# Three input loads of a fused RWKV-7 and gated-MLP kernel moved later: a of chunk 5 and b of chunk 4 into chunk 2, b of chunk 5 to the start of chunk 3

## The chip, the cores and the metric

The kernel runs on one core of a Trainium2 chip. The metric is the device time of one execution in microseconds; the kernel before takes 807.01 us (median of three runs, 802.86 to 811.95). The profile is that of one execution, which took 806.77 us. Times given as points, such as "at 86.40", count from the start of its span.

## What is computed

Two blocks run one after the other. The first is a recurrence over 768 time steps, for 4 batches and 8 heads with a head dimension of 40. The second applies two matrix products with x·cos(x) between them to the 3072 token rows that the first puts out.

```python
for t in range(S):
    y[:, :, t] = einsum('bhd,bhde->bhe', r[t], state)
    Sa = einsum('bhde,bhe->bhd', state, a[t])
    state = state * w[t][:, :, None, :] - einsum('bhd,bhe->bhde', Sa, b[t]) \
            + einsum('bhd,bhe->bhde', v[t], k[t])
x = y.transpose(0, 2, 1, 3).reshape(3072, 320)
h = x @ w_in                      # w_in 320 x 2048
out = (h * cos(h)) @ w_out        # w_out 2048 x 320
```

The two weight matrices arrive in double precision, as 8-byte words; the kernel turns them into float32 itself.

## The kernel before, in words

**Chunks.** The recurrence is cut into 24 chunks of 32 steps. A chunk `c` is five segments of `main(c)`, made at lines 921 to 927: `t` (`ch_t`: transposes the state, tile `sT`), `q` (`qps`), `x` (`x0ps`), `s` (`sps`) and `z` (`ch_z`: tile `dps`, then VectorE adds into the state `qz` at L754 and GpSimd multiplies it at L755). The next chunk's `ch_t` needs that `qz`. The three segments `v`, `k` and `g` of `p2(c + 1)` prepare the next chunk. `p1(c)` prepares w, a and b for a pair of chunks: `p1_w` (`pw`), `p1_a` (`pa`), `p1_b` (`pb`), `p1_n` (`pn`).

**Inputs.** Each input has one or two buffers in on-chip memory. `a`, `b` and `w` of chunk 4 go to the buffers that chunk 0 used, those of chunk 5 to the buffers of chunk 1; chunks 2 and 3 have places of their own, so these buffers are free long before chunk 1. `load(c, names)` (lines 146 to 152) issues four DMAs for each name, one for each batch, of 40 KB in runs of 160 bytes. All loads of this stage go through the queue of SyncE (SP), which works in program order: a DMA that waits holds up all behind it.

**Who reads the three loads.** `p1_w(4)`, which is `pw4`, the second segment of chunk 3, calls `over_w(4)`: VectorE takes the reciprocal of w (L395), then GpSimd multiplies b of chunk 4 by it (L396). `p1_a(4)`, which is `pa4`, transposes a of chunks 4 and 5 on TensorE (L330) and calls `over_w(5)`, whose product on GpSimd reads b of chunk 5.

**Weights.** `weights()` cuts the two matrices into 20 blocks of 128 x 512. Each block n goes through four steps (`rounded`, lines 224 to 266): fetch (L237, one to four DMAs on SP into a `words` buffer), taken (VectorE L245 and L246, ScalarE L249 and L251), mantissa (VectorE L255, ScalarE L258) and product (VectorE L261, GpSimd L264). The text below says F10 for the fetch of block 10, T10 for its "taken", M10 and P10 for the other two. From block 10 on there are three buffers in turn, so F10 can start once M7 has read block 7, F11 once M8 is done, F12 once M9 is done. The steps stand in one list, `w_steps`, of which each segment emits some after its own work: four in chunk 1, two in chunk 2, three in chunk 3. The order in the list around the change is P7, F10, M8, T9, P8, F11, M9, T10, P9, F12, M10, T11, P10 and so on.

**Order by hand.** The whole program is emitted in one order, and every engine runs its part of it in order. `step(work)` emits one segment; `later(n, work)` emits `work` behind the n-th step from then. In chunk 1 the steps are `t, F1, v, q, k, S1, x, g, s, z`; in chunk 2 `t, F2, v, q, S2, k, M, x, M, F3, g, M, s, S3, M, z, M, M`, where each M is a piece of the second block (`first_a`, `first_b` or `second`: tiles `ph` and `po`), and the F and S segments with numbers are small pieces of the recurrence (tile `below`). `busy` and `kept_busy` (tile `spare`) emit matmuls whose results nobody reads.

So in chunk 1 the SP queue holds, in this order behind the step named: w of chunk 5 and v of chunk 3 (`k`), a of chunk 5 and r of chunk 3 (`S1`), b of chunk 5 (`x`), F10 (`g`), b of chunk 4 and F11 (`s`), F12 (`z`). T10 stands behind step `s` on VectorE, and so ahead of the state updates L754 of chunk 1's `z`.

Of the kernel before, what the change touches and what calls it, by code (L numbers as in the profile page):

```python
# [20 lines left out]
def kernel(  # L21
# [124 lines left out]
    def load(c, names, via=nc.sync, parts=range(B)):  # L146
        for n in names:
            for i in parts:
                at_c = src[n][i, :, c * C : (c + 1) * C, :]
                if n == "w" and c >= 4:  # L150
                    at_c = wd[c // 4][i, :, c % 4]
                via.dma_start(nat[n, c][blk[i], :, :D], at_c.rearrange("h t d -> t h d"))  # L152
# [190 lines left out]
    def later(steps, work):  # L343
        waiting.append([steps, work])
# [201 lines left out]
    def pair_first(c, i, moe=True):  # L546
        ps = pair_space(c, moe, ps_h, "h")
        nt = G["noff"].rearrange("p c e j t -> p (c e j) t")
        half = pair_half(c, i)
        for n in range(H):  # L550
            for g in range(B):
                mm(
                    ps[blk[g], HB * n : HB * (n + 1)], nt[blk[g], H * i + n, :],
                    G["rn"][blk[g], H * i + n, :], n == 0,
                )
        nc.scalar.copy(half[:, :, :HB], ps[:, : H * HB].rearrange("p (n u) -> p n u", u=HB))
        if c + i == 3:
            nc.gpsimd.memset(padding(bn_b[6]), 0.0)
# [326 lines left out]
    def p1(c):  # L885


        def first_w():
            p1_w(c)
            if c == 4:  # L890
                later(1, lambda: load(6, "w"))

        def both_a():
            p1_a(c)
            if c == 4:
                later(1, lambda: load(7, "w"))
                for n in "ab":
                    for i in range(2):
                        later(1, lambda n=n, i=i: load(6 + i, n))
            elif c > 4 and c + 3 < NCH:  # L900
                for m in range(6):
                    later((9 if c == 6 else 2) + m, lambda m=m: load(c + 2 + m % 2, "wab"[m // 2]))

        return [first_w, both_a, lambda: p1_b(c), lambda: p1_n(c)]

    def scanned(q):

        ws_scan(q)
        later(2, lambda: ws_store(q))
        if q + 1 < NCH // 4:  # L910
            later(12, lambda: ws_fetch(q + 1))

    def p2(c):
        def last():
            p2_g(c)
            if c + 1 < NCH:
                later(4 if c == 1 else 1, lambda: p2_in(c + 1))

        return [lambda: p2_v(c), lambda: p2_k(c), last]

    def main(c):
        def last():
            ch_z(c)
            if c + 2 < NCH:
                later(8 if c == 2 else 1, lambda: p2_kn(c + 2))

        return [lambda: ch_t(c), lambda: ch_q(c), lambda: ch_x(c), lambda: ch_s(c), last]

    with tc.manual_schedule():
# [24 lines left out]
        def busy(n, after=False):  # L954


            ps = ps_h.tile([P, 512], F32, tag="h", name="busy")
            if after:
                nc.vector.memset(tick, 1.0)
                nc.tensor.matmul(  # L960
                    ps[:1, :], lhsT=tick, rhs=pick(idle, 0, (0, 4), (1, P)), start=True, stop=True, skip_group_check=True
                )
            for _ in range(n):
                mm(ps, idle, pick(idle, 0, (0, 4), (1, P)), True)
# [11 lines left out]
        def shifted(n):  # L976


            ps = at("pad")
            for _ in range(n):  # L980
                mm(ps[:1, 0, :1], idle[:, :1], idle[:, :1], True)
# [43 lines left out]
        busy(6)  # L1025
        step(z0, 0, 2)
        busy(4)
        for n, c, name in ((1, 4, "a"), (3, 4, "w"), (5, 5, "w"), (6, 5, "a"), (7, 5, "b"), (9, 4, "b")):
            later(n, lambda c=c, name=name: load(c, name))

        done = 0
# [17 lines left out]
        for c in range(NCH):  # L1049
            t, q, x, s, z = main(c)  # L1050
            v, k, g = p2(c + 1) if c + 1 < NCH else [lambda: None] * 3
            q0 = c - c % 4 + 4
            fill, pn, pn4 = (1, 4), None, None
            if c == 0:
                segs = []
            elif c == 1:
                segs, fill = [t, F1, v, q, k, S1, x, g, s, z], (1, 4)
            elif c == 2:
                segs, fill = [t, F2, v, q, S2, k, M, x, M, F3, g, M, s, S3, M, z, M, M], (0, 2)
            elif c == 3:  # L1060
                pw4, pa4, pb4, pn4 = p1(4)
                pw, pa, pb, pn = p1(6)
                segs = [
                    t, pw4, M, q, pa4, M, x, lambda: scanned(2), M, s, pw, M, pb4, pa, M, pn4, M, z, M,
                    pb, v, pn, k, M, g,
                ]
                fill = (2, 3)
            elif c == 4:
                pw, pa, *p8 = p1(8)
                firsts = [lambda n=n: pair_first(4, n) for n in range(4)]  # L1070
                seconds = [lambda n=n: pair_second(4, n) for n in range(4)]
                F4, F5, F6, F7 = firsts
                S4, S5, S6, S7 = seconds
                segs = [
                    t, v, M, q, M, k, x, M, F4, M, S4, F5, M, s, F6, M, pw, F7, M, z, M, g, M, pa, S5, lambda: scanned(3),
                ]
                fill = (2, 0)
            elif c == 5:
                pw, pa = p1(10)[:2]
                pb, pn = p8  # L1080
                segs = [t, M, pb, q, M, pn, k, M, x, M, s, S6, M, z, M, S7, M, pw, v, M, g, pa, M]
            elif c % 4 == 0 and q0 < NCH:
                pb, pn = p1(q0)[2:]
                segs = [t, v, M, q, M, k, x, M, g, M, s, pb, M, z, M, pn, M, M]
                if q0 + 4 < NCH:
                    segs.insert(-1, lambda: scanned(c // 4 + 2))
            elif c % 4 == 1 and q0 < NCH:
                pw, pa = p1(q0 + 2)[:2]
                segs = [t, M, pw, q, M, x, k, M, s, v, M, z, M, pa, M, g, M, M]
            elif c % 4 == 2 and q0 < NCH:  # L1090
                pb, pn = p1(q0 + 2)[2:]
                segs = [t, M, pb, q, M, pn, v, M, x, M, s, k, M, g, M, z, M, M]
            elif c % 4 == 3 and q0 + 4 < NCH:
                pw, pa = p1(q0 + 4)[:2]
                segs = [t, M, pw, q, M, x, k, M, s, v, M, z, M, pa, M, g, M, M]
            else:
                segs = [t, v, M, q, M, x, k, M, g, M, s, M, M, z, M, M]
            n = len(segs)

            goal = 8 * (c + 1) - (18 if c < 19 else 20)  # L1100
            empty, places = 0, segs.count(M)
            if c > 3:
                empty = max(0, min(places - (goal - done), 2 if c < 8 else places))
                goal = max(goal, done + places - empty)
            place = 0
            if c == 19:
                shifted(N_PAD[c])
            for i, seg in enumerate(segs):
                kept_busy(FILL.get((c, i), 0))
                while seg is s and ("rt", c) not in G:  # L1110
                    if allowed(c):
                        piece(4, 0)
                    else:
                        inv_steps.pop(0)()
                while seg is pn4 and w_steps:
                    w_steps.pop(0)()
                if seg is not M:
                    G["kind"] = "q" if seg is q and c > 3 else "other"
                    step(seg, *((0, 0) if c < 3 and seg in (*firsts, *seconds) else fill), small=seg in (q, x, g, s, z, pn, pn4, *firsts, *seconds))
                    if seg not in (*firsts, *seconds) and (c < 2 or c == 2 and not done):  # L1120
                        busy({s: 6, q: 5, v: 4, k: 4, z: 4}.get(seg, 3))
                else:
                    place += 1
                    if place * empty // places > (place - 1) * empty // places:
                        continue
                    if allowed(c) and (c != 4 or done < 23):
                        piece(*fill)
                while i == n - 1 and c > 3 and done < goal and c != 4 and allowed(c):
                    piece(*fill)
                if seg is pn and (c == 3 or c > 4 and c % 4 == 2):  # L1130
                    inv_steps.extend(by_blocks(q0) if c == 3 else inverse(q0))
# [36 lines left out]
```

## Time and profile before

| what | value |
|---|---|
| median of three runs | 807.01 us (802.86 to 811.95) |
| the profiled execution | 806.77 us |
| its span (first to last instruction) | 805.0 us |
| TensorE busy (PE) | 752.7 us, 94% of the span |
| VectorE busy (DVE) | 487.0 us, 60% |
| ScalarE busy (ACT) | 387.8 us, 48% |
| GpSimd busy (POOL) | 201.1 us, 25% |
| mean granted TensorE clock | 0.973 of full |
| SP's DMA queue | 52.11 MB, 30.1% of the 16 DMA engines' time |

The span is what the trace covers; the execution has 1.77 us around it. The profile's page cuts the span into 40 slices of 20.1 us. In the view "timeline" a line gives start, duration, engine, source line, operation, the tile written and the tiles read, a count, and in brackets the idle time of the engine before it with what ended it. "issue" there means a wait for nothing that the profile shows. SPq is SP's queue of DMA issues; its durations are those of issuing, not of the transfer.

### The profile page before, as it was taken

The numbers are of one execution on the slowest core, as the hardware profiler recorded it, in microseconds if no ns is written. First come the engines' busy times: TensorE is split into PE (matmuls) and PEld (weight loads), VectorE is DVE, ScalarE is ACT, GpSimd is POOL, SyncE is SP. The second block draws the span as 40 slices with busy tenths as digits, with TensorE's granted clock in tenths as the row PEclk, the third lists the DMA queues.
The fourth block names the chain that finished last, engine by engine and source line by source line (L and its number), as shares of the span: only waits on it lengthen the run. The fifth ranks groups of instructions, "written<-read, shape, count | busy, mean of one in ns | idle before, by whom it ended". The sixth has DMA issues, their size and how long they took to land.

```text
span 805.0 us, 39600 instructions
## 1 busy us (share of the span) xinstructions
PE 752.7 (94%) x17812; PEld 575.5 (71%) x17812; DVE 487.0 (60%) x1025; ACT 387.8 (48%) x723; POOL 201.1 (25%) x354
## 2 busy tenths in 40 slices
PE   5777698999999999999999999999999999999997
PEld 4544376777777777777777777777787777777775
DVE  8779658864734796553895644994346873333231
ACT  1337467555425435545435635535645445354352
POOL 5316535320322220330330230332131122201000
PEclk9688799999999999999999999999999999999999
DMA  8666552354253324334214314223220222101000
GB/s 114 176 162 149 143 145 74 57 121 65 59 125 58 66 38 71 72 92 67 60 40 69 94 36 72 53 45 69 46 46 21 46 46 49 24 17 34 19 17 16
DMA packets 183303, 55.78 MB, mean 69 GB/s; under 512 B 157152, under 2 KB 178656, under 8 KB 183136
## 3 DMA queue, kind: packets, MB, share of 16 engines
q1 hardware_dynamic: 177440, 52.11, 30.1%
q8 instruction: 140, 2.29, 1.2%
q10 hardware_dynamic: 5440, 0.82, 0.7%
q0 software_dynamic: 256, 0.33, 0.2%
q14 instruction: 27, 0.22, 0.1%
HBM read 42.07 MB, written 11.14 MB: 66 GB/s over the span
## 4 chain that ended last, share of the span: by engine, by line
PE 66%; DVE 18%; ACT 4%; issue 4%; DMA 3%; SPq 3%; POOL 1%; DVEq 0%; ACTq 0%; POOLq 0%
PE ph L101 23%; PE po L101 19%; PE x0ps L101 3%; PE dps L101 3%; SPq L152 3%; DVE inv_tmp L494 3%; DVE rw L395 3%; PE vT L330 3%; PE gram L101 2%; DVE inv L498 2%; PE sps L101 2%; PE nps L101 2%; PE qps L101 2%; PE sT L654 1%; DMA nat_a<-in_a_dram 1%
## 5 line engine op out<-in xcount | busy, mean ns | idle before, releaser
L101 PE MATMUL po<-w_out_sb,gT 128*128 128x320 f32 x768 | 223.1, 439 | 0.0
L101 PE MATMUL ph<-xT,w_in_sb 128*128 128x256 f32 x768 | 187.0, 388 | 0.3 <-issue 0.3
L101 PEld LDWEIGHTS po<-w_out_sb,gT 128*128 128x128 f32 x768 | 140.2, 190 | 54.2 <-issue 1.7
L101 PEld LDWEIGHTS ph<-xT,w_in_sb 128*128 128x128 f32 x768 | 140.1, 191 | 30.4 <-issue 12.5
L829 ACT ACTIVATE turns<-ph,rnd 128x512 f32<-128x512 f32 x96 | 64.1, 686 | 157.7 <-PE ph L101 157.3
L831 DVE SCALAR_TENSOR_TENSOR turns<-turns,ph 128x512 f32<-128x512 f32 x96 | 64.1, 685 | 111.7 <-ACT turns L829 111.4
L839 DVE TENSOR_TENSOR gT<-ph,turns 128x512 f32<-128x512 f32 x96 | 65.8, 687 | 39.1 <-ACT turns L836 39.1
L755 POOL TENSOR_TENSOR qz<-qz,wc 128x160 f32<-128x160 f32 x92 | 42.4, 480 | 167.1 <-DVE qz L754 166.5
L836 ACT ACTIVATE turns<-turns,half_pi 128x512 f32<-128x512 f32 x96 | 69.4, 723 | 3.1
L835 ACT ACTIVATE turns<-turns 128x512 f32<-128x512 f32 x96 | 60.2, 627 | 18.9 <-DVE turns L831 18.9
L101 PE MATMUL ph<-xT,w_in_tail 64*128 64x256 f32 (+1 forms) x512 | 54.9, 393 | 1.3 <-issue 1.3
L498 DVE TENSOR_TENSOR inv<-inv,inv_tmp 128x31 f32<-128x31 f32 (+15 forms) x124 | 51.2, 413 | 4.3
L754 DVE TENSOR_TENSOR qz<-dps,qz 128x160 f32<-128x160 f32 x92 | 29.2, 318 | 36.2 <-PE dps L101 36.0
L586 POOL COPY vp<-nat_v 128x320 f32<-128x320 f32 x24 | 11.9, 494 | 156.3 <-DMA nat_v<-in_v_dram 135.8
L494 DVE TENSOR_TENSOR inv_tmp<-u,inv 128x31 f32<-128x31 f32 (+15 forms) x124 | 48.6, 392 | 2.3
L395 DVE RECIPROCAL rw<-nat_w 128x320 f32<-128x320 f32 x20 | 42.9, 2144 | 0.1
L658 ACT COPY s<-sT 128x512 f32<-128x512 f32 x46 | 24.5, 585 | 35.1 <-PE sT L654 35.1
L101 PEld LDWEIGHTS ph<-xT,w_in_tail 64*128 64x128 f32 (+1 forms) x512 | 32.5, 160 | 10.4 <-issue 6.8
L766 POOL TENSOR_TENSOR yt<-yt,wb 128x512 f32<-128x512 f32 x24 | 31.9, 1329 | 22.3 <-DVE yt L761 22.3
L718 DVE TENSOR_TENSOR sm<-sps,su 128x128 f32<-128x128 f32 x48 | 11.7, 286 | 32.1 <-ACT sm L713 29.3
L396 POOL TENSOR_TENSOR bn<-nat_b,rw 128x320 f32<-128x320 f32 x22 | 20.1, 914 | 43.6 <-DVE rw L395 37.2
L642 ACT COPY vvm<-gram 128x256 f32<-128x256 f32 x24 | 8.8, 369 | 43.6 <-DVE ag L637 43.2
(136 smaller groups left out, 1127.9 us busy)
## 6 DMA issues: line engine op xcount, KB each, us to landing
words<-in_moe_w_in_dram SPq DMA_DIRECT2D x8, 512.0 KB
xd<-yt SPq DMA_DIRECT2D x48, 80.0 KB
out_dram<-ot SPq DMA_DIRECT2D x24, 160.0 KB
nat_k<-in_k_dram SPq DMA_DIRECT2D x92, 40.0 KB
nat_v<-in_v_dram SPq DMA_DIRECT2D x92, 40.0 KB
nat_r<-in_r_dram SPq DMA_DIRECT2D x92, 40.0 KB
nat_a<-in_a_dram SPq DMA_DIRECT2D x84, 40.0 KB
ws<-in_w_dram SPq DMA_DIRECT2D x5, 640.0 KB
```

The costliest lines, as they stand in the source:

```text
L101: nc.tensor.matmul(o, lhsT=lhsT, rhs=rhs, start=start, stop=stop, skip_group_check=True)
L395: nc.vector.reciprocal(rw, wn)
L494: nc.vector.tensor_tensor(tmp, u[:, j : j + 1, :j].to_broadcast([P, C - j, j]), x[:, j:, j : j + 1].to_broadcast([P, C - j, j]), ALU.mult,)
L498: nc.vector.tensor_tensor(x[:, j:, :j], x[:, j:, :j], tmp, ALU.subtract)
L754: nc.vector.tensor_tensor(z, pick(dp, 0, (2 * N72 + C, 2), (N72, 2), (1, D)), z, ALU.add)
L755: nc.gpsimd.tensor_tensor(z, z, wc.rearrange("p (f m b) -> p f m b", f=2, m=2)[:, :, :, bb] .unsqueeze(3).to_broadcast([P, 2, 2, D]), ALU. ...
L766: nc.gpsimd.tensor_tensor(yt.rearrange("p j b t -> p (j b) t"), yt.rearrange("p j b t -> p (j b) t"), wx, ALU.mult)
L829: nc.scalar.activation(n, u, ACTF.Identity, bias=rnd, scale=1.0)
L831: nc.vector.scalar_tensor_tensor(n, n, -ROUND, u, ALU.add, ALU.subtract)
L835: nc.scalar.activation(n, n, ACTF.Abs)
L836: nc.scalar.activation(n, n, ACTF.Sin, bias=half_pi, scale=-2.0 * math.pi)
L839: nc.vector.tensor_tensor(gT[:, 2 * e : 2 * e + 2].rearrange("p f t -> p (f t)"), us[e], ns[e], ALU.mult)
```

## The change

Of the six loads that were registered ahead of chunk 1, three stay there. Load a of chunk 5 and b of chunk 4 are registered at the start of chunk 2, to be emitted behind its steps 11 (`g`) and 14 (`S3`). Load b of chunk 5 is registered at the start of chunk 3, to be emitted behind its first step (`t`). Nothing else is touched: each DMA is the same as before, and so is every instruction of the other engines.

```diff
-        for n, c, name in ((1, 4, "a"), (3, 4, "w"), (5, 5, "w"), (6, 5, "a"), (7, 5, "b"), (9, 4, "b")):
+        for n, c, name in ((1, 4, "a"), (3, 4, "w"), (5, 5, "w")):
             later(n, lambda c=c, name=name: load(c, name))
...
             elif c == 2:
+                for n, m, name in ((11, 5, "a"), (14, 4, "b")):
+                    later(n, lambda m=m, name=name: load(m, name))
                 segs, fill = [t, F2, v, q, S2, k, M, x, M, F3, g, M, s, S3, M, z, M, M], (0, 2)
...
                     pb, v, pn, k, M, g,
                 ]
+                for n, m, name in ((1, 5, "b"),):
+                    later(n, lambda m=m, name=name: load(m, name))
                 fill = (2, 3)
```

## The prediction, made before the changed kernel was run

> **What bounds the kernel now.** I read the page first. TensorE is busy 94% of the span, so the change can only pay where TensorE stands still. The slices show where: from the sixth slice on PE stands at 9 but for the seventh and the last, and the clock is full. The slack lies in the first 100 us.
>
> ```profile
> PE   5777698999999999999999999999999999999997
> ...
> PEclk9688799999999999999999999999999999999999
> ```
>
> The fifth slice (80.5 to 100.6 us) has the lowest clock after the second. The chain of waits crosses it on a DMA: 5.80 us from 86.40, F10 from memory to its buffer, and 38.7% of the chain between 84 and 99 us. So I read the timeline of VectorE, then of SP, then of TensorE there.
>
> ```profile
> 86.20 0.87 DVE L255 SCALAR_TENSOR_TENSOR mant<-words,mant 128x512 f32<-128x512 uint32 x1
> 92.30 0.43 DVE L245 TENSOR_SCALAR mant<-words 128x512 int32<-128x512 int32 x1 [5.22 <-DMA words<-in_moe_w_in_dram]
> ...
> 93.58 0.32 DVE L754 TENSOR_TENSOR qz<-dps,qz 128x160 f32<-128x160 f32 x1
> ```
>
> VectorE ends M9 at 87.07 and then stands for 5.22 us in T10, waiting for F10. Behind T10 stands L754, the state update of chunk 1, on which chunk 2 depends.
>
> ```profile
> 75.81 3.16 SPq L152 DMA_DIRECT2D nat_v<-in_v_dram  x4
> 79.06 3.28 SPq L152 DMA_DIRECT2D nat_a<-in_a_dram  x4
> 82.38 1.93 SPq L152 DMA_DIRECT2D nat_r<-in_r_dram  x4
> 84.41 1.89 SPq L152 DMA_DIRECT2D nat_b<-in_b_dram  x4
> 86.40 0.39 SPq L237 DMA_DIRECT2D words<-in_moe_w_in_dram  x1
> 86.88 1.88 SPq L152 DMA_DIRECT2D nat_b<-in_b_dram  x4
> 88.86 4.46 SPq L237 DMA_DIRECT2D words<-in_moe_w_in_dram  x5
> ```
>
> SP issues without a break from 75.81 to 90.96, and the view of SP's waits shows none between 75 and 90 us. F10 is the fifth line. Its buffer was free when M7 ended, at 79.03; it went out at 86.40 because a of chunk 5 and b of chunk 5 stand ahead of it. (The chain puts a VectorE instruction of step `s` before F10; that is emitted after F10, so F10 can't wait for it. It only ended at the same moment.)
>
> ```profile
> 88.02 0.82 PE L101 MATMUL busy<-idle 128*128 128x512 bf16 x3
> 92.48 0.38 PE L101 MATMUL busy<-idle 128*128 128x512 bf16 x1 [3.64 <-issue]
> ...
> 96.35 1.89 PE L654 MATMUL sT<-ident,qz 128*128 128x128 f32 x6 [0.29 <-POOL qz L755]
> 98.04 1.48 PE L101 MATMUL busy<-idle 128*128 128x512 bf16 x3
> ```
>
> TensorE, too, has a wait here that isn't for F10: 3.64 us of "issue", up to 92.48. The trace has a 16 KB packet on the instruction queue at 89.66, 0.90 us long, so I read it as a wait for instructions. From 98 us on TensorE is full again until 126.
>
> **What the Trainium skill says.** "DMA: Bandwidth & Descriptors", section "Issuing engines are not separate DMA queues": all DMAs run on the same 16 engines; another issuer saves only issue time. The trace agrees as to the term that matters here, the issue time: about 0.49 us for each DMA of 40 KB. "Runtime: NRT & Kernel Launch", section "Instruction fetch mechanics": instructions come in 16 KiB blocks of 256 over a DMA queue of the engine's own, "mostly hidden". The page's queue 8 agrees in size (140 packets, 2.29 MB), but 3.64 us at 88.84 are not hidden. "TensorE: Matmul & The Clock Gate", section "Part 1: The HAM clock gate": the clock halves after an idle window of about 3.4 us, and a busy one restores it. The clock records agree: half from 93.3 to 100.1, two such windows, behind the gap of 88.84 to 95.37.
>
> **The change part by part.**
>
> (1) *Eight issues ahead of F10 go.* a: 79.06 to 82.34, b: 84.41 to 86.30. One of the eight took 1.85 us (79.50), just when a 16 KB instruction packet was on an engine (79.49, 1.47 us). That packet comes anyhow and will hold up r of chunk 3, which moves into that place. So 8 x 0.49 = 3.9 to 4.0 us; F10 goes out at 86.40 - 4.0 = 82.4. If the long issue went with a, it would be 5.4 us. I take 4.0.
>
> (2) *F10 lands earlier.* 5.80 us after issue as before: 88.2. In the landing events 15 of its 16 parts are in at 90.63, 4.2 us after issue; only one lags to 92.20, behind the instruction packet of 89.66. Between 82.4 and 87 the trace has no such packet, so 4.2 us are possible: 86.6. VectorE is ready at 87.07. Its wait of 5.22 falls to between 0 and 1.1; gain 4.1 to 5.2, I take 4.6.
>
> (3) *F11, F12 and b of chunk 4.* b of chunk 4 (1.88 us) goes from between F10 and F11. F11 then waits for M8 (83.35) and goes at 83.4 instead of 88.86; F12 follows M9 at 87.1 instead of 89.3. T11 and T12 come 4.6 us earlier (91.3 and 95.0). F16, also of 512 KB, landed 5.5 us after its issue: F11 in at 88.9; F12 by about 93. Cost 0. If F12 were late, VectorE has idle stretches of 1.92 us (105.4) and 3.33 us (110.9) before TensorE needs it.
>
> (4) *The clock.* At half clock the last six `sT` took 1.89 us, 0.315 each; chunk 3's eight took 1.04, 0.13 each: 1.1 us. Three `busy` took 1.48 instead of 0.82: 0.66. `below` and `vT` add 0.2 or so. If the gap shrinks enough to spare both half windows this is worth 1.9, if not 0 (a second half window elsewhere would take it back). I take one of the two: 1.0.
>
> (5) *a of 5 and b of 4 in chunk 2.* Here are SP's lines of chunks 2 and 3:
>
> ```profile
> 114.37 1.95 SPq L237 DMA_DIRECT2D words<-in_moe_w_in_dram  x2
> 121.54 6.95 SPq L237 DMA_DIRECT2D words<-in_moe_w_out_dram  x5
> ...
> 141.07 7.79 SPq L152 DMA_DIRECT2D nat_w<-wd  x8
> ```
>
> On the old time scale, a's four issues fall between F16 (114.37) and F17 (116.00): F17 goes about 1 us later, and T17 reads it only at 130.5, after it landed at 121.1. b's four fall between F17 and F18, where SP waits until 121.54 for M15. Both lie in idle time of SP: cost 0. Their readers come at 140.7 (transposes) and 141.08 (GpSimd), 15 us later. Without this cover it would be 8 x 0.49 = 3.9 us of SP, not of TensorE.
>
> (6) *b of 5 in chunk 3.* Four issues (2.0 us) after `xT`, whose issues end at 136.55: from 136.6 to 138.6; SP otherwise waits there until 141.07 for the reciprocal. Landed by 140.6, since the next load on SP, issued at 141.07, has its first part in at 142.91. Its reader:
>
> ```profile
> 146.49 0.87 POOL L396 TENSOR_TENSOR bn<-nat_b,rw 128x320 f32<-128x320 f32 x1 [2.16 <-DVE rw L395]
> ```
>
> 5.9 us of cover, so cost 0. If it failed, GpSimd would wait with the products for k and v of chunk 5 (147.32) behind it.
>
> Sum: 4.6 + 1.0 = 5.6 us. 805.0 - 5.6 = 799.4 of span, plus 1.77 around it, 801.2; the median stands 0.24 above the profiled execution: 801.4. All later work is in program order and TensorE is full, so I expect the gain to be carried to the end.
>
> **Rivals.** *The stall goes and more with it* (0.30). All of (2) and (4) come, 5.2 + 1.9 = 7.1, and the program, 7 us earlier, meets instruction packets and clock windows differently: the "issue" waits at 123.31 (0.34) and 126.48 (1.27), the one at 231.01 (1.34) with the half window from 233.2 (3.4 us, so 1.7 of loss) hold 4.6 us, of which half: 9.4 us, 797.6. For it: these waits lie in stretches with dense DMA. Against it: the moved loads now add to that traffic.
>
> *TensorE's own wait takes the place* (0.18). If the instructions still come at 92.48, TensorE does 0.9 us of `busy` and `spare` and starts `sT` at 93.4 instead of 95.37, and ends eight of them at half clock (8 x 0.315 = 2.5) at 95.9 instead of 98.24: 2.3 us, 804.7. For it: the packet of 89.66 began 0.8 us after TensorE had run dry, where most others began before, so dense DMA delayed it, and F11 will now be in flight there. Against it: the queue is thinner by 12 DMAs.
>
> *Slower: the loads in chunk 2 hold up TensorE's instructions* (0.10). TensorE is full from 100 to 126, with instruction packets at 112.44, 117.69, 121.25 and 125.14, which are nearly hidden today. a and b put 2048 small packets beside the first three. If each of these cost what 88.84 cost, 3 x 3.64 = 10.9 less the 5.6 gained is 5.3, and one more half clock window 1.7: 814.0. It decides from 5.6 / 3.64 = 1.5 such waits on. Against it: 40 KB loads run beside these fetches at 103 to 112 us already, and TensorE shows no such wait there.
>
> **How the numbers follow.** The main case, the sum, has 0.42; its own range, with a median's scatter (the runs spread from 802.86 to 811.95), is 799 to 804. The four together give a range of 796 to 806.5: it takes in the second and third case and leaves out the slower one and the tail of the best. 1% is 8.07 us, about what a measurement of this kernel can tell from no change. Below 798.9 are three quarters of the second case and a quarter of the main one: 0.34. Above 815.1 is half of the slower case and some scatter: 0.08. Within 1%: 0.58.
>
> **What would show it.** Right: F10 on SP at 82 to 83; VectorE's wait before T10 under 1.2 us; `sT` of chunk 2 4 to 6 us earlier; no wait for b of 5 on GpSimd (L396), none for F17. Wrong: F10 no earlier than 85, or the wait moved to T11 or T12; TensorE's "issue" wait still ending near 92.5; new "issue" waits between 108 and 122; or the lead of chunk 2 gone by 160 us.

## The result, and the profile after

The changed kernel takes 802.25 us (median of 22 runs, 798.85 to 806.68); the kernel before, run beside it, 806.85 us (802.44 to 811.95). The ratio is 0.9954, 95% interval 0.9935 to 0.9972: 4.6 us less by the medians, 3.7 by the ratio. The profiled execution is one of the kernel's longer ones: 805.37 us, span 803.7. Of all executions in this document one alone, of e9 below (1394.74 us), counts as slow, and e9's ratio leaves it out.

The page shows as good as nothing of the change; the clock row has lost a low slice, the fifth (80.4 to 100.5 us):

```profile
PE   4777799999989999999999999999999999999997
...
PEclk9778999999999999999999999999999999999999
```

SP's timeline: a and b of chunk 5 are gone from between r of chunk 3 and F10, and F10 leaves at 81.03 (86.40 before). By the landing events the last of its 16 parts is in 3.97 us after that (5.80 before). The six issues of F10, F11 and F12 stand in one line, since nothing lies between them now.

```profile
77.99 2.94 SPq L152 DMA_DIRECT2D nat_r<-in_r_dram  x4
81.03 8.60 SPq L237 DMA_DIRECT2D words<-in_moe_w_in_dram  x6
```

VectorE's timeline: T10 starts at 86.57, right behind M9, where it stood for 5.22 us before. The state update L754 follows at 88.10 (93.58 before).

```profile
85.77 0.88 DVE L255 SCALAR_TENSOR_TENSOR mant<-words,mant 128x512 f32<-128x512 uint32 x1
86.57 0.67 DVE L245 TENSOR_SCALAR mant<-words 128x512 int32<-128x512 int32 x1
...
88.10 0.32 DVE L754 TENSOR_TENSOR qz<-dps,qz 128x160 f32<-128x160 f32 x1
```

TensorE's timeline: the "issue" wait ends at 90.12 (92.48 before), and all eight `sT` run in 1.39 us. Before, the last six alone took 1.89.

```profile
87.58 0.82 PE L101 MATMUL busy<-idle 128*128 128x512 bf16 x3
90.12 0.38 PE L101 MATMUL busy<-idle 128*128 128x512 bf16 x1 [1.72 <-issue]
90.33 0.66 PE L101 MATMUL spare<-idle 128*128 128x192 bf16 x6
90.82 1.39 PE L654 MATMUL sT<-ident,qz 128*128 128x128 f32 x8
92.06 0.81 PE L101 MATMUL busy<-idle 128*128 128x512 bf16 x3
```

The moved loads, on SP in chunk 2: a of 5 stands between F16 and F17, b of 4 between F17 and F18.

```profile
108.67 0.36 SPq L237 DMA_DIRECT2D words<-in_moe_w_in_dram  x1
109.14 3.37 SPq L152 DMA_DIRECT2D nat_a<-in_a_dram  x4
112.61 0.38 SPq L237 DMA_DIRECT2D words<-in_moe_w_in_dram  x1
113.09 4.10 SPq L152 DMA_DIRECT2D nat_b<-in_b_dram  x4
117.29 6.23 SPq L237 DMA_DIRECT2D words<-in_moe_w_out_dram  x5
```

GpSimd's reader of b of 5 waits for the reciprocal as before (2.15 us, 2.16 before), not for the load:

```profile
141.44 0.86 POOL L396 TENSOR_TENSOR bn<-nat_b,rw 128x320 f32<-128x320 f32 x1 [2.15 <-DVE rw L395]
```

The lead over the first trace of before, read at the same matmul of both: 6.0 us at the end of chunk 2's `sT`, 5.0 at the end of its `dps`, 2.6 at chunk 4's and 1.1 at the end. In this execution two waits of TensorE that are 0.34 and 0 in the first trace of before eat most of it, each with a half clock window of 3.4 us behind it (118.8 and 170.0):

```profile
118.38 2.17 PE L101 MATMUL ph<-xT,w_in_sb 128*128 128x256 f32 x5 [1.92 <-issue]
...
168.90 0.51 PE L101 MATMUL gram<-aT,kT 40*32 40x32 f32 x37 [1.47 <-issue]
```

### The profile page after: what moved, and what is told of

The parts are those of the page before. It is cut to its first block, busy times and chain, and to the rows that moved or that the text cites. A ratio compares the mean times of both kernels' runs of the same rounds, so it can differ in the third digit from the quotient of the medians.

```text
span 803.7 us, 39602 instructions
## 1 busy us (share of the span) xinstructions
PE 753.0 (94%) x17812; PEld 578.6 (72%) x17812; DVE 487.9 (61%) x1025; ACT 387.2 (48%) x723; POOL 200.2 (25%) x354
## 4 chain that ended last, share of the span: by engine, by line
PE 68%; DVE 14%; ACT 5%; DMA 5%; issue 4%; POOL 2%; SPq 2%; DVEq 0%; ACTq 0%; POOLq 0%
PE ph L101 24%; PE po L101 20%; PE x0ps L101 4%; PE dps L101 3%; DVE rw L395 3%; PE gram L101 3%; PE vT L330 3%; PE sps L101 2%; DVE inv_tmp L494 2%; DVE inv L498 2%; PE nps L101 2%; PE qps L101 2%; PE sT L654 1%; SPq L152 1%; PE kT L330 1%
## 5 line engine op out<-in xcount | busy, mean ns | idle before, releaser
L754 DVE TENSOR_TENSOR qz<-dps,qz 128x160 f32<-128x160 f32 x92 | 28.9, 314 | 35.5 <-PE dps L101 35.4
```

## The experiments

What happens before chunk 1's `dps` moves by almost 4 us from one trace to another (its last matmul ends at 87.2 to 91.1 us in the fourteen traces). So the place is measured from there: "place" is the time from the end of chunk 1's last `dps` to the end of chunk 2's last `sT`, and "chunk 2" that from the end of chunk 1's `dps` to the end of chunk 2's. "Packet" is the start of TensorE's 16 KB instruction packet against the end of chunk 1's `dps`, by the DMA packets of the trace. Several values are several traces (of the kernel before the first and e10, of the changed one the first, e1 and e12); each trace is one execution. Ratios are to the kernel before, on the same chip.

That the "issue" wait is a wait for this packet can be seen across the traces: in the thirteen that have it, the wait ends 1.0 to 1.9 us after the packet's end, wherever the packet stands.

| kernel | VectorE waits for F10 | packet | TensorE's issue wait | place | chunk 2 | ratio (95%) |
|---|---|---|---|---|---|---|
| before | 5.22, 5.08 | +1.57, -1.12 | 3.64, 0.71 | 10.15, 9.30 | 40.0, 39.0 | 1 |
| changed | 0, 0, 0 | -0.15, -0.40, -1.11 | 1.72, 0.54, 0 | 4.58, 4.57, 3.84 | 35.5, 35.3, 33.7 | 0.9954 (0.9935-0.9972), 0.9952 (0.9930-0.9974) |
| e2: loads behind F10 | 0 | +1.93 | 4.19 | 8.13 | 37.0 | 0.9982 (0.9964-1.0000) |
| e5, e11: behind F10 and F11 | 0, 0 | +1.07, +0.55 | 3.09, 2.54 | 6.05, 6.30 | 37.5, 37.4 | 1.0009 (0.9991-1.0027) |
| e9: ten tiny DMAs ahead of F10 | 4.72 | -0.39 | 1.45 | 9.35 | 40.5 | 1.0002 (0.9980-1.0023) |
| e3: b of 4 ahead too | 4.34 | -0.45 | 1.45 | 8.98 | 41.1 | 1.0034 (1.0015-1.0053) |
| e4: only b of 4 moved | 2.95 | +1.89 | 3.37 | 7.89 | 37.6 | 1.0007 (0.9982-1.0031) |
| e8: only b of 5 moved | 0.48 | +3.11 | 5.29 | 9.29 | 39.4 | 1.0008 (0.9990-1.0026) |
| e6: a and b later in chunk 2 | 0 | -0.23 | 1.45 | 4.56 | 34.1 | 0.9958 (0.9934-0.9982) |
| e7: a behind F17 | 0 | -0.40 | 1.45 | 4.57 | 34.3 | 0.9955 (0.9938-0.9972) |

**e1, the changed kernel again.**

> The changed kernel once more, for a second trace. Measure of the place: time from the end of chunk 1's last dps matmul to the end of chunk 2's sT (10.15 us before, 4.58 in the first trace of the change). Theory (F10 stood behind eight issues on SP): again 4.3 to 5.5 us, VectorE waits under 1 us for F10, time 0.993 to 0.998 of before. Theory on the tail (the lead of 6 us at chunk 2 is worn down later by instruction-fetch waits that fall at random): the places where the lead shrinks differ from the first trace (118.4 and 168.9 there), and the lead at the end lies anywhere from 1 to 7 us. Rival on the tail (the moved loads themselves cause the wait at 118.4): an issue wait of 1 to 2 us between 112 and 122 is there again.

Ratio 0.9952, place 4.57, no wait of VectorE for F10: as the theory had it. The waits at 118.4 and 168.9 are both there again (1.80 at 120.07, 1.58 at 171.23). So this trace speaks for the rival on the tail, not for chance; e12 below changes that.

**e2, the order alone.**

```diff
-(1, 4, "a"), (3, 4, "w"), (5, 5, "w"), (6, 5, "a"), (7, 5, "b"), (9, 4, "b")
+(1, 4, "a"), (3, 4, "w"), (5, 5, "w"), (9, 4, "b"), (10, 5, "a"), (11, 5, "b")
```

> All three loads stay by chunk 1, but behind F10: b of 4 ahead of F11 as before, a of 5 ahead of F12, b of 5 behind chunk 2's first step. Theory (order on SP): F10 goes out as in the changed kernel (81 to 83), the measure of the place is 4.3 to 6 us, time 0.993 to 0.998 of before, the same as the changed kernel within 0.3%. Rival (it is the thinner traffic in chunk 1 that helps): F10's way or the instruction packet behind it stays slow, measure 7 to 10 us, time as before within 0.2%. If the loads in chunk 2 cost TensorE its wait at 118.4, this kernel has none there and is up to 0.3% faster than the changed one.

The theory failed. VectorE no longer waits, but TensorE's own wait takes the place: it stands until 94.40, then does the eight `sT` at half clock. The ratio is 0.9982 and the place 8.13, both in the rival's ranges. It is the third case of the prediction, which had put 2.3 us on it; at the place it is 2.0. (The interval of e2 and those of the changed kernel just overlap.)

```profile
94.40 0.53 PE L101 MATMUL busy<-idle 128*128 128x512 bf16 x1 [4.19 <-issue]
94.72 1.16 PE L101 MATMUL spare<-idle 128*128 128x192 bf16 x6
95.69 1.91 PE L654 MATMUL sT<-ident,qz 128*128 128x128 f32 x8
```

The instruction packet started at 91.39, after the 4 KB packets of F10 and F11 (84.60 to 90.98). In the changed kernel these were over by 87.46, and the instruction packet started at 87.49. No wait stands near 118 here, which fits the loads in chunk 2 making it; the time gained nothing by that.

**e3, three loads ahead of F10.**

```diff
-(7, 5, "b"), (9, 4, "b")
+(7, 5, "b"), (7, 4, "b")
```

> The opposite: b of 4 goes ahead of F10 too, so 12 issues stand before it instead of 8. Theory (order on SP, 0.49 us an issue): F10 at 88.4, VectorE waits 7.2 us in T10, the measure of the place 12.1 us (10.15 + 2.0), time 1.001 to 1.005 of before. Rival (thinner traffic): same traffic, same time, measure 10 us.

The kernel is longer by 0.34%, within what the order would have. But the mechanism that was expected isn't what the trace shows. F10 did go out 2.0 us later behind v of chunk 3 (9.38 us after the end of v's issues, 7.43 before), yet it was read 4.1 us after its issue, not 5.9, so VectorE's wait is shorter than before (4.34) and the place too: 8.98, not 12.1. Chunk 2 is longer all the same (41.1), with three half clock windows in a row (93.1 to 103.3) where the two traces of before have two. Where the 0.34% comes from is thus not shown. VectorE's line:

```profile
91.54 0.43 DVE L245 TENSOR_SCALAR mant<-words 128x512 int32<-128x512 int32 x1 [4.34 <-DMA words<-in_moe_w_in_dram]
```

**e4, b of 4 alone.**

```diff
-(6, 5, "a"), (7, 5, "b"), (9, 4, "b")
+(6, 5, "a"), (7, 5, "b")
 ...
+                for n, m, name in ((14, 4, "b"),):
```

> Only b of 4, which stands behind F10, moves to chunk 2; a and b of 5 stay ahead of F10. Theory (order on SP): F10 at 86.4 as before, VectorE waits 5 us, measure of the place 9.5 to 10.5 us, time 0.998 to 1.002 of before. Rival (thinner traffic helps F10 and the instruction packet behind it): measure 7 to 9 us, time 0.996 to 0.999.

No gain in time (1.0007). The place is in the rival's range (7.89), the time is not. F10 was read 4.5 us after its issue, not 5.9. That b no longer stands behind it need not be the reason: in e8 b does, and F10 was read after 4.4. TensorE's own wait (3.37) then ends only 0.9 us before its `sT`, where it ended 2.9 us before in the first trace of before.

**e5, the loads behind F10 and F11.**

```diff
-(5, 5, "w"), (6, 5, "a"), (7, 5, "b"), (9, 4, "b")
+(5, 5, "w"), (10, 4, "b"), (10, 5, "a"), (11, 5, "b")
```

> All three loads by chunk 1, but behind F10 and F11 both: b of 4 and a of 5 stand between F11 and F12, b of 5 behind chunk 2's first step. Theory now (TensorE's instruction packet waits behind the 512 KB of F10 and F11; the 160-byte loads don't hold it): F10 and F11 go out together as in the changed kernel, their 4 KB packets are over before TensorE asks, measure of the place (end of chunk 1's dps to end of chunk 2's sT) 4 to 6 us, TensorE's issue wait under 2.2 us, time 0.991 to 0.996 of before. Rival (the small loads in chunk 1 hold the instruction packet): measure 7.5 to 10 us as in the kernel with the order changed alone, time 0.997 to 1.000.

This theory failed too, as to time wholly. The packets of F10 and F11 are over at 89.63, and still the instruction packet starts only at 90.94, with b of 4 and a of 5 issued from 85.64 to 90.67. So the packet is late with small loads queued, too, as the rival had it; the place, 6.05, lies between the two ranges. TensorE's timeline:

```profile
93.71 0.38 PE L101 MATMUL busy<-idle 128*128 128x512 bf16 x1 [3.09 <-issue]
```

The place gives 1.5 us of the change's gain back, chunk 2 gives 2.0; the median gives all 4.6 back. Where the other 2.6 go no trace shows.

**e6 and e7, the loads elsewhere in chunk 2.**

```diff
-((11, 5, "a"), (14, 4, "b"))
+((16, 5, "a"), (17, 4, "b"))      # e6
+((13, 5, "a"), (14, 4, "b"))      # e7
```

> The changed kernel with a of 5 and b of 4 later in chunk 2, behind steps 16 and 17, where SP waits between F18 and F19. Theory (a of 5 ahead of F17 puts F17 onto TensorE's instruction packet and makes the wait at 118): no issue wait over 0.6 us between 112 and 121, no half clock there, chunk 2's dps ends 2 to 3 us earlier against chunk 2's sT than in the changed kernel (30.7 and 30.9 us there, 29.9 before at a clock that was half at first), time 0.990 to 0.995 of before. Rival (that wait comes by chance of position): it is there again, time as the changed kernel, 0.995.

> The changed kernel with a of 5 behind step 13 instead of 11, so behind F17 instead of ahead of it; nothing else. Theory: F17 follows F16 within 1.7 us instead of 3.9, no issue wait over 0.6 us between 112 and 121, time 0.990 to 0.995 of before. Rival (chance of position, or the small loads themselves): the wait of 1.8 to 1.9 us is there again and the time is that of the changed kernel.

In both traces the wait at 118 is down to 0.39 and 0.55, and chunk 2 is 0.9 to 1.4 us shorter than in the first two traces of the change. Of e6, 2 to 3 us were expected. The ratios, 0.9958 and 0.9955, miss the 0.990 to 0.995 that were expected and are not better than the changed kernel's. So the theory fits where the wait stands in these two traces, and nothing of it can be seen in the time. In the third trace of the change (e12), with a of 5 ahead of F17, chunk 2 is shorter still (33.7).

**e8, b of 5 alone.**

```diff
-(6, 5, "a"), (7, 5, "b"), (9, 4, "b")
+(6, 5, "a"), (9, 4, "b")
```

with b of 5 at the start of chunk 3 as in the change.

> Only b of 5 moves, to chunk 3; a of 5 stays ahead of F10, b of 4 between F10 and F11. Theory: F10 goes out 2.0 us earlier (84.4 on the scale of before) but F11 only behind b of 4, so the 4 KB packets still lie on TensorE's instruction packet: VectorE waits 2 to 3.5 us for F10, TensorE's issue wait ends as late as before, measure of the place 7.5 to 10 us, time 0.997 to 1.001. Rival (half of the issues, half of the gain): measure 7 to 7.7 us, time 0.9970 to 0.9985.

No gain (1.0008). VectorE's wait fell more than expected, to 0.48, but the packet came 3.11 us behind `dps` and TensorE stood for 5.29 us: half of the change brings nothing, not half.

```profile
94.29 0.58 PE L101 MATMUL busy<-idle 128*128 128x512 bf16 x1 [5.29 <-issue]
```

(The traced execution, 810.31 us, is the longest of this kernel's 22; the ratio is of all of them.)

**e9, issue time without traffic.**

```diff
+    scrap = const.tile([P, 10], F32, tag="scrap", name="scrap")
+    def tiny(lo, n):
+        for i in range(lo, lo + n):
+            nc.sync.dma_start(scrap[:16, i : i + 1], r[0, 0, :16, i : i + 1])
 ...
+        for n, lo in ((6, 0), (7, 5)):
+            later(n, lambda lo=lo: tiny(lo, 5))
```

> The changed kernel with ten DMAs of 64 bytes each put where a and b of 5 stood ahead of F10; nobody reads what they bring. They cost SP its issue time (about 0.4 us each, 4 us) and next to no traffic: F10 is late as before, the loads are out of the stretch as in the changed kernel. Theory (both are needed: F10 early, and nothing queued on the DMA engines when TensorE asks for instructions): F10 goes out about 4 us later than in the changed kernel, VectorE waits 3.5 to 5 us for it, F10 and F11 lie on the instruction packet; measure of the place (end of chunk 1's dps to end of chunk 2's sT) 8 to 10.5 us, time 0.998 to 1.001 of before. Rival (thin traffic alone brings the gain): measure under 7 us, time 0.9955 to 0.997.

The gain is gone: 1.0002. Ten DMAs of 64 bytes cost SP 4.6 us (0.46 each; the kernel's lines stand six further down), and VectorE waits for F10 again. SP's timeline, then VectorE's:

```profile
86.97 2.31 SPq L186 DMA_DIRECT2D scrap<-in_r_dram  x5
89.38 4.40 SPq L243 DMA_DIRECT2D words<-in_moe_w_in_dram  x6
```

```profile
93.91 0.43 DVE L251 TENSOR_SCALAR mant<-words 128x512 int32<-128x512 int32 x1 [4.72 <-DMA words<-in_moe_w_in_dram]
```

The one part that the theory had wrong: F10 and F11 (from 90.37) did not lie on the instruction packet, which was earlier (89.82), and TensorE's issue wait was 1.45. It then waited 3.70 us for the state. This kernel, too, has a of 5 ahead of F17, and both of the later waits: 1.86 us at 126.02 (`ph`) and 1.95 at 177.02 (`gram`).

**e10, e11, e12: second and third traces.**

> The kernel before once more, for a second trace. If the reading of its first trace is no accident: VectorE waits 4.5 to 6 us for F10, TensorE's issue wait after chunk 1's dps is 3 to 5 us, measure of the place 9 to 10.5 us, chunk 2 (end of dps of chunk 1 to end of dps of chunk 2) 38.5 to 40.5 us.

VectorE's wait for F10 is there again, TensorE's issue wait is down to 0.71, where 3 to 5 us were expected, with the packet 1.12 us ahead of the end of `dps`. So of the two waits in the kernel before the one for F10 is in both traces; the other comes and goes beneath it. F10's last part again landed late, 5.42 us after its issue. VectorE's line, then TensorE's:

```profile
94.44 0.43 DVE L245 TENSOR_SCALAR mant<-words 128x512 int32<-128x512 int32 x1 [5.08 <-DMA words<-in_moe_w_in_dram]
```

```profile
93.12 0.38 PE L101 MATMUL busy<-idle 128*128 128x512 bf16 x1 [0.71 <-issue]
```

> The kernel with the three loads behind F10 and F11 once more, for a second trace, since its first trace had gained 2.5 us in chunk 2 while its median had gained nothing. If small loads queued on the DMA engines hold TensorE's instruction packet: again a packet that starts 1 us or more after the end of chunk 1's dps, an issue wait of 3 us or more, measure of the place 6 to 8.5 us. If the first trace's wait was an accident: packet before the end of dps as in the changed kernel, measure 4.3 to 5.5 us.

Place 6.30, packet 0.55 us behind the end of `dps`, issue wait 2.54: nearer to the first reading than to an accident, with the packet and the wait below what was named for it.

> The changed kernel a third time, for the tail. Both its traces have an issue wait of 1.5 to 1.6 us in chunk 3's last gram (at 169 and 171 us) with a half clock window behind it, and both executions (805.37 and about 806.5 us) lie above the kernel's median of 802.3. Theory (that wait comes and goes from one execution to another, by whether the instruction packet starts before or behind the 640 KB of ws): if this execution takes 800 to 803.5 us, its trace has no issue wait over 1 us there and 674 to 677.5 us from the end of chunk 2's dps to the end of the span (680.5 and 679.7 in the two before); if it takes 805 us or more, the wait is there. Rival (the changed kernel always has it): it is there in an execution of 800 to 803.5 us too. Measure of the place: 4.3 to 5.0 us in either case.

800.58 us. No issue wait at the last `gram` of chunk 3, and 674.7 us from chunk 2's `dps` to the end, against 680.5 and 679.7 (676.9 and 674.4 in the two traces of before); the lead over the first trace of before is 5.9 us at the end. The wait at 118 is absent as well, but in its place the next one, at the last `dps` of chunk 2, is 1.85 us (at 123.80; 0.16 and 0.45 in the other two traces of the change, 1.27 and 1.33 before). So both come and go in the changed kernel, which takes back what e1 seemed to say. The place was 3.84, below what was expected, since TensorE had no issue wait at all. Here are the place and, below it, the last `dps` of chunk 2:

```profile
90.43 1.64 PE L101 MATMUL busy<-idle 128*128 128x512 bf16 x4
...
123.80 0.36 PE L101 MATMUL dps<-sm,bn 32*40 32x72 f32 x14 [1.85 <-issue]
```

Whether the moved loads have a part in the wait at chunk 3's `gram` stays open. It is 1.2 to 2.0 us long in five of the eight traces of kernels that have a load moved to the later steps of chunk 2 or to chunk 3 (the first two of the change, e4, e8, e9), and at most 0.41 in the six traces of the others. No experiment was made on it.

## Why the prediction was right

**The time.** 801.4 was forecast, 802.25 measured; a gain of 5.6 against 4.6 by the medians (3.7 by the ratio), inside the main case's own range. Within 1% was the likeliest class. The sum was right at the place and a little too large at the end, and one thing that it needed was not in it (the third case, below).

**Steps 1 and 2 hold.** F10's issue behind v of chunk 3 came 4.35 us sooner (3.08 us after the end of v's issues instead of 7.43; 4.0 forecast), the long issue stayed and moved to r, and VectorE's wait fell from 5.22 to 0: the gain was 5.2, the upper end; 4.6 was taken. F10 left at 81.03, ahead of the 82 to 83 that were named, since the issues ahead of it ran 1.0 us earlier in this trace. It landed 3.97 us after its issue; 4.2 was called possible. The reason given, that the instruction packet held back one part, stays open: in e9 such a packet is in flight beside F10 too, and the last part lags the fifteenth by 0.56 us, in e3 by 0.13, against 1.57 and 1.45 in the two traces of before. e9 shows that the issue time is a cause and not a companion: the same delay without the loads' traffic takes the whole gain away.

**Step 3 holds**: no wait in T11 or T12.

**Step 4, the clock.** In the first trace of the change the clock is full from 81.2 to 118.8; in the second there is one half window at 89.8, in the third one at 87.7. None of the three goes to half clock at its `sT` or just behind it; the two traces of before do, for two windows, from 93.3 and from 95.6. At the place the change is worth 10.15 - 4.58 = 5.57 us by the first traces, 9.30 - 4.57 = 4.73 by the second ones, against 5.6 in the sum.

**Step 5 was too cheap.** It costed a of chunk 5 ahead of F17 at nothing, since T17 comes so late. F17 went out 3.9 us behind F16 instead of 1.6, not 1 us later, and in two of three traces TensorE waited 1.8 to 1.9 us for instructions beside it (e9 makes it three of four; in the ten traces with nothing ahead of F17 this wait is at most 0.63). A new wait between 108 and 122 was one of the signs of being wrong, and it came. It looks like the mechanism of the fourth case, with half its price per wait and only in some executions; but it is only in part an added cost, since the wait at the last `dps` is 0.8 to 1.2 us shorter in those two traces than before. That the load ahead of F17 makes it is not shown, and e6 and e7 don't show it in the time.

**Step 6 holds**: b of 5 cost nothing.

**"Carried to the end"** is right for the median and wrong for single executions: the lead at the end was 1.1, 0.2 and 5.9 us in the three traces. That lead also holds what came before the place. From the end of chunk 1's `dps` to the end of the span it is 716.0, 714.9 and 708.4 us in the changed kernel and 717.0 and 713.4 before, so that traces alone would not tell the two kernels apart; the medians do. In the first two traces most of what was lost went to the waits near 118 and 169 us, with the half clock windows behind them.

**The third case** named what the prediction had left too small. It had argued that the thinner queue would spare TensorE's own wait, as a reason against a rival, and priced nothing for it; but it is half of the cause. Step 2 takes its whole gain on to `sT`, which holds only if TensorE's own wait ends earlier too, and no step says why it should. That it did was luck as far as the sum goes. With F10 early and the loads left close by (e2, e5), the gain is 0.2% or nothing; with the loads away and F10 late (e9), nothing. Neither alone brings a gain that is clear of noise: the best of them is e2, with 0.18% and an interval that reaches 1. Two waits stood in parallel ahead of one `sT`, and both have to go. The need for both is shown by the times of e2, e5 and e9; how the loads make the packet late is argued from the traces alone. All six traces with the three loads away have it before the end of `dps`, but so have two of the eight with all or some of them close by (e10 and e3).

**What stays open.** Why e5 loses 4.6 us in its median where its traces account for 2. Why e3 is longer. Whether the waits in chunks 2 and 3 belong to the moved loads. And the exact queueing: the instruction packet starts later with data queued on the DMA engines in the first trace of before and in e2, e4, e5, e8 and e11, but not in e3, where small loads are in flight around its start (87.76), nor in e10; and when TensorE asks for it the trace does not say, so the delay itself is not measured.

## What to carry to other kernels

Where a wait ends on a DMA, look at what the issuing queue did before it, and then at what the waiting engine's consumer would wait for next: here a second wait, for instructions, lay beneath the first and took its place as soon as only the first was removed. Small loads that have 50 us to spare still cost what stands behind them in a queue that is issuing without a break: 0.46 to 0.49 us each here, for 64 bytes as for 40 KB. A saving of half a per cent can't be read from one trace: the lead at the end was 1.1 us in one execution and 5.9 in another of the same kernel.

## What the runs showed of the hardware that was not expected

Ten DMAs of 64 bytes took SP about as long as loads of 40 KB do: 0.46 us each (0.47 to 0.49 for those). Long issues on SP go with TensorE's 16 KB instruction packets: between 60 and 150 us the fourteen traces have 144 issues that took over 0.9 us (up to 2.4), and every one overlaps such a packet; of the 1242 shorter ones, 143 do. TensorE's wait for one 16 KB instruction packet was between 0 and 5.29 us at the same instruction, and the packet itself took only 0.9 to 2.1 us; in six of the eight traces with all or some of the loads close by it started 0.55 to 3.11 us behind the end of `dps`, in the other eight traces 0.15 to 1.12 ahead of it. The 512 KB fetch F10 was read between 4.1 and 5.9 us after its issue in those kernels where VectorE stood waiting for it. Of its 16 parts the last landed 5.8 and 5.4 us after issue in the two traces of before, 3.9 to 4.4 in the other twelve.
